# DeltaNet and MLP on one core: a new written order of all steps, decodes that wait for both transfers, and an early square root

## The chip, the cores and the metric

The kernel runs on one core of a Trainium2 chip. The time is the device time of one execution in microseconds. Its engines are TensorE (PE, matrix products; PEld are its weight loads), VectorE (DVE), ScalarE (ACT), GpSimd (POOL) and SyncE (SP); SP, ACT and POOL also issue DMA transfers. Each engine runs its instructions in the order in which the program holds them.

## What is computed

Two blocks follow each other. The first is a DeltaNet recurrence over 768 positions for 4 x 8 heads of 48 dimensions; the second is a layer norm and a two-layer MLP with a residual, on rows of 384 numbers.

```
k_n = k / (np.linalg.norm(k, axis=-1, keepdims=True) + 1e-06)
for t in range(S):
    y[:, :, t] = np.einsum('bhd,bhde->bhe', q[:, :, t], state)
    v_old = np.einsum('bhde,bhd->bhe', state, kt)
    state = state + bt * np.einsum('bhd,bhe->bhde', kt, vt - v_old)
...
x = attn_out.transpose(0, 2, 1, 3).reshape(B, S, H * D)
xn = (x - mu) / np.sqrt(var + 1e-06) * g_ln
out = x + np.maximum(xn @ w_ch1, 0.0) @ w_ch2
```

All data is float32. q, k, v and beta come in as (4, 8, 768, ...); w_ch1 is 384 x 1536, w_ch2 is 1536 x 384.

## The kernel before

**Tiling.** The 768 positions are cut into 12 chunks of 64. In a chunk the recurrence is a product with the inverse of a triangular 64 x 64 matrix, one for each of the 32 heads, and the state is carried from chunk to chunk. Chunk c has a recurrence (`recur`, tag c0, c1, ...) and then an MLP over its 256 rows (`mlp`, tag m0, m1, ...). Chunks 2 and 3, 4 and 5, and so on get their inverses in pairs by a substitution on VectorE (`rows_inverse`, tags x1, x2, ...; half of chunk 1 likewise, tag x0). From chunk 3 on, PE runs the MLPs with fewer products, whose sums are made on DVE, ACT and POOL.

**The start.** Chunk 0 cannot wait for VectorE's substitution: `first_inverse` makes its inverse on PE by doubling, in five levels, each for two groups of heads. A level has a product E (L771, with `qt` and `gsb`), a masked copy of E on DVE (L776), a product Z (L786, with `xt`), a transpose of Z on DVE (L735), and three back copies of Z on ACT (L729); the next E needs the transposes, the next Z the back copies. Ahead of them the keys of chunk 0 (`kr`, four transfers) are squared on ACT (L654), summed (L655) and rooted (L656) for the norms, turned on PE (L628), copied on ACT (L633) and multiplied with each other (L695). The results of E and Z go in turn to the PSUM tiles `two`, `by`, and the pair f0 and f1. After the inverse come the recurrence of chunk 0 (L1069, L1074, L1095), its output copy (L1133), the layer norm (L1139 to L1189), and the first product of the MLP, L1407. Gram products (L819) for chunks 1, 2 and 3 and the queries lie in between.

**Weights.** Both weight matrices come as pairs of 32-bit words and are put together on the chip. A piece is fetched by two transfers of 384 KB each, issued by ACT (`fetch`, keys "wd"), into one of five buffers (`words`, or a part of `h_all`). `convert` then decodes it in four operations: ACT scales the high words (L584), DVE shifts them (L589), ACT scales the low words (L592), POOL adds (L602). There are 12 pieces; the first three are decoded in two halves, which stand half by half in the two transfers.

**The order.** The function first records some 2,900 steps (`add`: engine, a cost, a closure, the keys it reads and writes). Then `emit` goes through ORDER, a list of step numbers written into the file, and emits each step as it comes; it only asserts that a step's inputs were emitted before. So ORDER alone sets the order on each engine, and the transfers' too: those that SP and ACT issue take their turns with eight semaphores in ORDER's order, so that one must have landed before the eighth after it can be issued. An "f" in ORDER is a filler: a product of zeros into the upper half of bank f0 (`zeros`, L1582). The three fills at the beginning (L617) are steps.

Of the kernel before, what the change touches and what calls it, by code (L numbers as in the profile page):

```python
# [131 lines left out]
47 9 6 257 8 48-49 10-11 13 1 32 26 23 14 0 12 65 7 66 60 39-43 256 45-46 44 61 55 74 53-54 52 58-59 327 56-57 63  # L132
405 408 64 37 21 5 17 30 71 35 73 69 75 238 79-80 82 85-86 96 89 88 36 29 15-16 20 4 18-19 90 33 97 87 91-92 3 93
98-99 83 100 94 84 101 81 106 104-105 103 76 38 27 95 102 124 22 125 118 126 239 119 24 77 108 70 107 109-110 215 78
226 127 111 122 121 112 129 72 246 123 240 128 213 133 25 134 120 f f 130 31 114 28 131-132 f f 135-137 141 115 2
142-143 222 139 138 140 147-150 216 145 230-231 146 144 157 151 116-117 214 159 153 152 158 209-210 163 250 154-155
161-162 160 156 211 164 113 401 403 314-316 412 260 325 67 313 326 265 410 259 262 68 264 263 266 261 413-414 328
407 409 212 f f 168 165 227 166-167 248 232 218 172-173 171 174 318 228 178 249 170 169 175-176 317 180-183 241 233
229 217 251 320 177 319 179 242 244 267 224 234 f 185 321 184 186 191 268-269 50 192 34 270-271 187 273 258 272 638
245 193 274-279 219 280 f f 197 243 322 370 329 323 188 195 330 189-190 331 194 196 247 369 332 363 650 652 399 199  # L140
198 200-201 205 333 204 364 202-203 206-207 334 208 335 f f f f 339 337 281-290 235 223 291-296 338 297-298 340 299
252 300-301 51 302-303 62 640 225 469 400 f 341-342 371 343-344 361-362 236-237 642 654 347 253 348 365 352 f f 435
434 402 324 404 336 411 304 474 477 406 476 475 307 305 767 309-310 312 308 311 306 437 436 345-346 353 372 349-351
354 220 373 367 221 374 f f f 438 355 359 439 360 366 440 415 357-358 356 478 577 575 254 578 581 479 368 255
480-482 418 416 473 484 643 641 637 644 656 649 655 639 653 768-769 771 773 772 770 766 419 576 375-376 579 614 420
580 583-584 379 377 582 388 381-382 421 485-503 422 504-509 378 510 423 511 645 587 615 585 616-617 387 588 591 424
586 592 428 427 426 595-596 425 417 380 651 589 429 441 599 618-619 442 774 512-523 394 430 433 431 590 383 432 393
443-444 385 389 445 593 524-526 390 657 527-528 448 446-447 384 529 600-602 646 908 449-450 391 397 395 1052 1054
1064 386 530 453 531 454 451-452 392 1066 603 647 604 658 620-621 594 458 455 605-606 597 607 659 456 532-533 459
534 460 457 461 465-466 464 467-468 463 462 598 622-623 608 396 535 483 398 1068 1065 536-539 629 540 630 541 631  # L150
542-543 632 544-547 633 609 778 775 805 624 610 625 806 910 912 763 907 911 764 914 901 648 913 660 909 900 662 1160
663-665 915 776 548 1056 1051 1057 1055 666 765 906 661 611 626 667-670 672 1162 550 549 551 903 552 628 627 673-674
902 905 1163 904 1165 1157 1167 613 811-812 807 777 809 817 810 818 675-677 815 808 816 823 821-822 824 813-814 1070
1069 829 832 830 833 1067 1053 678 779 679-690 553 691-701 554-558 838 819 702-704 634 705-706 564 707-711 559 827
839-840 562 561 560 563 828 820 780 841-842 848-849 843 781 712 1063 831 835 845 836 713 784 782 714 565 786 785 567
844 789 787 783 790 834 1058 825 850 715 788 568 826 794 791 566 569 795 716-717 796 792 718-719 793 720 855-856
851-852 865 916 853-854 801 797 570 866 846 873 867 837 802 799 804 574 572 571 800 573 803 798 917 721 1059 1526
847 1525 918 722-723 920 724 635 725-728 857 868 874-875 869 876 919 921 870 858 877 859-860 729-730 636 731-735
1347 1166 1348 1155-1156 1164 612 1168 736 1169 922-923 871 861 880-883 671 924 1071 1060 878-879 925 1061 1072
471-472 470 862 1528 1538 1170 1161 863-864 954 948 1073 927 891-893 956-957 884 894 872 926 895 962 896 1171 897  # L160
885 960 930-931 935 963 968 928 936 929 1540 1530 949 1075 951 950 739-740 1352 1062 1074 737-738 1077 1076
1078-1079 1172 886 969 961 932 937 741 1173 742 745-746 1080 958-959 743 974-975 744 887-888 955 980 953 933 952 752
1175 939 934 1081-1084 1087 1086 1529 1541 1531 1527 1537 1539 1532 1088-1091 938 1092-1104 966 989 747 967 749 964
748 965 751 972 990-993 750 973 970 1174 753 971 978 976 979 999-1001 994-995 1176 977 755-756 754 757 1177 1354 899
1356 889 898 890 1351 1345 1353 1158 940 1344 1159 941 1346 942 944 1357 943 1355 1006-1008 981 986 996 1016 1002
1009 1003 1010 983-984 982 1204 985 1203 987-988 1542 998 997 1014 1004 1017 1011 758 761 759 947 945 1178 1180 1018
1105-1109 1085 1110-1117 1005 1118-1119 946 762 760 1630 1358-1359 1637 1211 1120-1121 1179 1639 1629 1640-1641 1349
1122-1126 1024-1026 1212 1027-1029 1213 1019-1021 1030 1022 1543 1013 1023 1012 1182 1360 1031 1127 1350 1222 1015
1218 1185 1128 1361 1186 1129 1205 1226 1042 1032-1033 1043 1034-1036 1362 1130 1181 1190-1191 1183 1223 1037 1215
1044-1047 1216 1363 1184 1364 1131 1365 1132 1192 1133 1187 1214 1048 1217 1039 1206 1544 1366 1219 1227 1224 1220  # L170
1367 1369 1245 1230 1246 1231 1207-1208 1221 1533 1188 1134 1194 1189 1193 1368 1135 1225 1545 1232 1228 1534 1239
1233 1038 1209 1264 1259 1254 2026 1210 1240 1229 1535 1241 1234 1136 1242 1137-1138 1243 1247-1248 1250 1249 1251
1244 1139-1140 1252 1141-1142 1546 1265 1255 1266 1143-1145 1253 1547 1195 1643 1197 1642 1536 1636 1198 1638 1196
1049 1040 1199 1050 1548 1146 1267 1147-1148 1260-1261 1256 1149 1257 1262 1258 1202 1268 2028 2014 1273 1269
1235-1236 1292 1270 1293 1237 1274 1276 1271 1644 1275 1282-1283 1238 1272 1201 1277 1279 1403 1399 1289 1278 1280
1284-1288 1263 1200 1294 1645 1299-1302 1295-1297 1303-1304 1041 1150 1549 1298 1317 1309 1318 1553 1552 1829 1551
1550 1290 1392 1281 1305 1396 1310 1319-1320 1554 1291 1307 1306 1311 1321-1322 1312 1555 1646 1556 1308 1313-1314
1393 1557 1315 1558 1561 1323 1394 1316 1560 1407 1830 1828 1633 1151 1822 1154 1153 1152 1831 1833-1834 1832 2120
1835 1634 1324-1329 1335-1337 1330 1338-1339 1397 1340 1400-1401 1562-1563 1370 1372 1564-1565 1371 1566 1373-1376
1341 1377 1395 1408-1409 1379 1410 1402 2027 1635 1567 1404 1380 1568-1570 1378 1571 1405 1658 1416 1411 2015 1435  # L180
1445 1381 1423-1424 1572 1398 1406 1420-1421 1412 1426 1413-1414 2030 1427 1440 2029 1331-1332 2013 2016-2017 1422
1573 1647 1574 1382 1415 1648 1431 1651 1650 1649 1652 1428 1432 1429-1430 1575 1383 1425 1576 1660 1577 1433
1578-1580 1436 1653 1656 1654-1655 1441 1417 1442 1437 1446 1581 1447 1582 1418 1448 1438 1657 1449 1439 1659
1661-1662 1419 1450 1454 2025 1457 1455 1443 1583 1836 1343 1384 1334 1385 1387 1631 1333 1632 2125 1386 2126 1463
1451 1464-1468 1452 1584-1588 1453 1458-1459 1456 1460 1665 1663 1589 1469 1444 1434 1473-1475 1461 1470-1471 1462
2118 2117 1388 1342 2122 2124 2121 1821 2127 1390 1389 1391 1590 1480 1476-1477 1481 1478 1591 1664 1839 1592 1479
1472 1593-1595 1559 1482-1484 1498-1499 1490 1500-1501 1491-1493 1485 1502 1494-1495 1487 2032 2018 1596-1598 1496
1599 1688 1837 1503 1505-1507 1600 1486 1838 1699 1497 1827 1695 2031 1488-1489 2019 1666 1504 1668 1667 1601-1602
1689 1508-1509 1692 1510 1516 1690 1603 1511 1670 1669 1671 1840 1842 1604 1850 1696-1697 1517-1518 1693 1707 1703
1708 1731 2020 1675 1843-1844 1672 1841 1691 1845 1519-1521 1704-1705 1846 1849 1847-1848 1851 1706 1698 1605 1852  # L190
1606-1608 1676 1853-1854 1694 1673 1609-1612 1677 1522 1679 1674 1613-1614 1678 1615 1700-1702 1616 2021 1719-1720
1824 1826 1825 2129 2119 1823 1855 1680 2128 1512 1722 1741 1513 1709 1716 1710 1723 1736 1717-1718 1856 1617-1618
# [1537 lines left out]
```

## Time and profile before

| what | us |
|---|---|
| runs of the kernel | 529.24 median, 527.1 to 530.44 |
| the profiled execution | 530.82 |
| its span, first to last instruction | 529.1 |
| its granted PE clock | 0.976 of full |
| first product of the keys (L695) | 17.87 |
| first Z of the inverse (L786) | 29.74 |
| second Z, last group starts | 35.12 |
| third Z, first group | 42.56 |
| fifth Z, last group starts | 58.94 |
| first output copy of chunk 0 (L1133) | 65.75 |
| first MLP product (L1407) | 75.18 |
| last PE product ends | 524.7 |

How to read the lines that follow in the prediction. On the page, a line of an engine gives its busy time, its share of the span and its instructions. The rows of digits cut the span into 40 slices of 13.2 us; each digit is a busy share in tenths (9 is 90% or more), and PEclk is the clock that PE was granted, in tenths. The chain of waits follows the work that ended last back to the beginning; in order of time its lines give start, length, and what it was. A line of the waits gives who waited for whom, the sum, how often, and the longest. A line of the timeline gives start, length, engine, line of the code, operation, output and inputs, shape, how many; in brackets stands the idle time before it and what ended it.

### The profile page before, as it was taken

How to read it: one execution, taken by the hardware profiler on the slowest of the kernel's cores; microseconds unless marked ns; L12 is line 12 of the kernel's file. 1: busy time of each engine (PE TensorE's matmuls, PEld its weight loads, DVE VectorE, ACT ScalarE, POOL GpSimd, SP SyncE). 2: the span in 40 equal slices, each digit the busy share in tenths (PEclk: the TensorE clock that was granted, in tenths of full speed). 3: DMA queues.
4: the chain of work that ended last, by engine and by line, in shares of the span. 5: the costliest groups of instructions: out<-in, count | busy, mean ns of one | idle time of the engine just before them, and what ended most of it. 6: DMA issues, size and time to landing. Idle time of an engine off the chain costs nothing.

```text
span 529.1 us, 22717 instructions
## 1 busy us (share of the span) xinstructions
PE 496.1 (94%) x9938; PEld 451.6 (85%) x9938; DVE 358.6 (68%) x819; ACT 207.2 (39%) x451; POOL 284.3 (54%) x447
## 2 busy tenths in 40 slices
PE   5667988999999999989999999999999999999996
PEld 2455776767888889979999999999999999999996
DVE  2547778878997599986899954998837436354241
ACT  1786562542442334233261452353423424424130
POOL 7004485447245967767649437346374362554644
PEclk9588899999999999999999999999999999999999
DMA  9876759749543893159357267234343502102011
GB/s 178 200 161 122 211 89 233 118 121 164 101 69 81 178 156 55 35 147 191 60 120 135 48 184 126 45 85 75 97 100 71 117 4 60 34 33 59 1 32 30
DMA packets 181635, 54.56 MB, mean 103 GB/s; under 512 B 164888, under 2 KB 177312, under 8 KB 181536
## 3 DMA queue, kind: packets, MB, share of 16 engines
q1 hardware_dynamic: 168512, 40.10, 37.9%
q10 hardware_dynamic: 10816, 9.83, 6.7%
q0 software_dynamic: 2208, 3.17, 3.6%
q8 instruction: 78, 1.28, 1.0%
q14 instruction: 21, 0.17, 0.1%
HBM read 36.30 MB, written 16.78 MB: 100 GB/s over the span
## 4 chain that ended last, share of the span: by engine, by line
PE 85%; DVE 5%; issue 3%; DMA 2%; ACT 2%; SPq 1%; ACTq 0%; POOL 0%; DVEq 0%
PE f L1504 28%; PE f L1307 22%; PE f L1407 9%; PE two L819 3%; PE f L1429 3%; PE f L1582 2%; PE by L1033 2%; PE by L1095 2%; PE two L1088 2%; PE two L1033 2%; PE two L1105 2%; DVE xb L914 1%; DMA words<-in_moe_w_ch_dram 1%; SPq L401 1%; DMA kr<-in_k_dram 1%
## 5 line engine op out<-in xcount | busy, mean ns | idle before, releaser
L1504 PE MATMUL f<-w_sb,h_all 128*128 128x192 f32 x396 | 81.8, 329 | 0.0
L1491 POOL TENSOR_TENSOR h_all<-h_all 128x256 f32<-128x256 f32 x99 | 72.9, 753 | 14.9 <-DVE tmp L907 6.1
L1504 PE MATMUL f<-words,h_all 128*128 128x192 f32 x396 | 78.4, 330 | 0.1
L1330 DVE TENSOR_TENSOR h_all<-f,h_all 128x512 f32<-128x512 f32 x72 | 49.1, 686 | 33.3 <-PE f L1307 25.4
L1529 POOL TENSOR_TENSOR words<-h_all 128x128 f32<-128x128 f32 x66 | 31.2, 491 | 70.0 <-ACT h_all L1334 34.2
L1504 PEld LDWEIGHTS f<-w_sb,h_all 128*128 128x128 f32 x396 | 65.3, 190 | 1.1 <-POOL h_all L1491 0.2
L1504 PEld LDWEIGHTS f<-words,h_all 128*128 128x128 f32 x396 | 64.8, 190 | 1.4 <-issue 0.2
L914 DVE TENSOR_TENSOR xb<-xb,tmp 128x31 f32<-128x31 f32 (+19 forms) x139 | 58.8, 423 | 3.1
L907 DVE TENSOR_TENSOR tmp<-xb,gb 128x31 f32<-128x31 f32 (+19 forms) x139 | 53.0, 381 | 4.0 <-POOL xb L894 0.6
L1407 PE MATMUL f<-xnt,w_sb 128*128 128x256 f32 x216 | 52.6, 391 | 0.3 <-issue 0.3
L1325 ACT COPY h_all<-f 128x512 f32<-128x512 f32 x45 | 26.0, 586 | 58.8 <-PE f L1307 41.0
L401 POOL DMA_DIRECT2D tb<-in_k_dram x64 | 42.0, 660 | 13.0 <-DVE xb L914 7.4
L1334 ACT ACTIVATE h_all<-h_all 128x512 f32<-128x512 f32 x54 | 32.3, 625 | 36.2 <-DVE h_all L1330 36.0
L1407 PEld LDWEIGHTS f<-xnt,w_sb 128*128 128x128 f32 x216 | 40.4, 192 | 7.0 <-ACT h_all L1416 0.4
L1307 PE MATMUL f<-x_new,w_sb 128*128 128x128 f32 x288 | 39.8, 277 | 1.3 <-DVE h_all L1330 1.1
L1307 PE MATMUL f<-xnt,w_sb 128*128 128x128 f32 x288 | 40.7, 277 | 0.0
L1522 DVE TENSOR_TENSOR o<-f,x 128x192 f32<-128x192 f32 x33 | 11.6, 354 | 41.7 <-PE f L1504 24.9
L602 POOL TENSOR_TENSOR w_sb<-words 128x768 uint32<-128x768 uint32 (+1 forms) x11 | 15.0, 1365 | 43.3 <-DVE words L589 33.4
L1307 PEld LDWEIGHTS f<-x_new,w_sb 128*128 128x128 f32 x288 | 36.7, 192 | 1.7 <-issue 1.5
L1307 PEld LDWEIGHTS f<-xnt,w_sb 128*128 128x128 f32 x288 | 37.1, 191 | 0.3
L1133 ACT COPY x<-by 128x384 f32<-128x384 f32 x23 | 10.4, 481 | 53.2 <-POOL o L1522 36.3
L1416 ACT ACTIVATE h_all<-f 128x256 f32<-128x256 f32 x36 | 13.4, 383 | 35.1 <-PE f L1407 34.9
(252 smaller groups left out, 987.4 us busy)
## 6 DMA issues: line engine op xcount, KB each, us to landing
words<-in_moe_w_ch_dram ACTq DMA_DIRECT2D x20, 384.0 KB, 4.6
gd<-gsb SPq DMA_DIRECT2D x11, 512.0 KB, 3.9
v<-in_v_dram SPq DMA_DIRECT2D x24, 192.0 KB, 3.9
kr<-in_k_dram SPq DMA_DIRECT2D x46, 96.0 KB, 3.6
out_dram<-o SPq DMA_DIRECT2D x46, 96.0 KB, 2.3
xld<-xlt SPq DMA_DIRECT2D x9, 384.0 KB, 2.5
xnt<-xld SPq DMA_DIRECT2D x36, 96.0 KB, 3.0
tb<-in_q_dram SPq DMA_DIRECT2D x40, 64.0 KB, 2.9
```

The lines of the kernel that those rows point to most:

```text
L401: add(eng, cost, lambda: QUEUE[eng].dma_start(out=out_, in_=in_), r, w, bulk=n * ns / 16e3, np=n, **kw)
L907: lambda j=j, n=n, w=w, t=t: nc.vector.tensor_tensor(out=t, in0=xv[:, 0:n, j : j + 1].to_broadcast([128, n, w]), in1=gv[:, j : j + 1, j + ...
L914: "DVE", dve(n * w), lambda t=t, rest=rest: nc.vector.tensor_tensor(out=rest, in0=rest, in1=t, op=ALU.subtract),
L1033: nc.tensor.matmul(dst[half(e), hp, j], src[drows(hp), (e if n else key_half(c, hp, e)) * GP + j], s_all[drows(hp), e, j], start=(n == 0 o ...
L1307: nc.tensor.matmul(wide(p[:, f : f + 128]), w[:, f : f + 128], r, start=start and i == 0, stop=True, skip_group_check=True)
L1325: add("ACT", act(512), lambda: nc.scalar.copy(o, p), pk, ok)
L1330: add("DVE", dve(512), lambda: nc.vector.tensor_tensor(out=o, in0=x, in1=y, op=op), [*xk_, *yk], ok)
L1334: add("ACT", act(512), lambda: nc.scalar.activation(o, o, ACTF.Relu, scale=scale), [], ok)
L1407: nc.tensor.matmul(p[:, 0:TOK], w1_sb[:, t, f * 128 : (f + 1) * 128], xnt[:, t], start=(t == 0), stop=(t == KC - 1))
L1491: add(eng, cost, lambda: e.tensor_tensor(out=out_, in0=x, in1=y, op=op), r, w, port=2 if eng == "Pool" else 1, pr=-2)
L1504: lambda f=f, t=start and f == order[0]: nc.tensor.matmul(p[:, 0:D2], lhs(f), rhs[:, f], start=t, stop=(f == order[-1]), skip_group_check=True
L1529: lambda f=f + i: e.tensor_tensor(out=s3[f], in0=one(0, 0)[0](f), in1=one(1, 0)[0](f), op=ALU.subtract),
```

## The change

Three things change in the recorded steps. The memset of `eps` and its square root, a step whose only use is that ACT loads its table, are recorded first, and the first steps on ACT that don't issue a transfer now need it (key "act"). A decode needs both transfers of its piece, also where it decodes one half. And ORDER is another list.

```
+    c_dve(lambda: nc.vector.memset(eps, 1e-6), 0.06, ["eps"])
+    add("ACT", 1.48, lambda: nc.scalar.sqrt(rstd[:, 0, 0:1], eps), ["eps"], [("ln", 0, 0), "act"], t0=2.2)
     c_dve(lambda: nc.vector.memset(nought, 0.0), 0.2, ["nought"], pr=-300)
...
                     "ACT", act(512), lambda o=o: nc.scalar.copy(o, eye[:, None, :].to_broadcast([128, H, C])),
-                    ["eye"], [(*key, x) for x in range(2)],
+                    ["eye", "act"], [(*key, x) for x in range(2)],
...
-    c_dve(lambda: nc.vector.memset(eps, 1e-6), 0.06, ["eps"])
-    add("ACT", 1.5, lambda: nc.scalar.sqrt(rstd[:, 0, 0:1], eps), ["eps"], [("ln", 0, 0)], t0=2.2)
...
-        wk = WORD_KEYS[BUF[i]] + [("wd", BUF[i], c0 // 384 + y) for y in range(n // 384)]
+        wk = WORD_KEYS[BUF[i]] + [("wd", BUF[i], y) for y in range(2)] + ["act"]
...
-            add("ACT", act(512), lambda o=o, i=i: nc.scalar.copy(o, i), pair[2 + g], [dkey + (g,)], **kw)
+            add("ACT", act(512), lambda o=o, i=i: nc.scalar.copy(o, i), [*pair[2 + g], "act"], [dkey + (g,)], **kw)
...
-            add("ACT", act(384), lambda sq=sq, s=s: nc.scalar.square(sq, kn[:, s]), raw_keys(0), kg, **kw)
+            add("ACT", act(384), lambda sq=sq, s=s: nc.scalar.square(sq, kn[:, s]), [*raw_keys(0), "act"], kg, **kw)
```

Each engine keeps the same operations, but ACT has one load of its function table where it had two, and there are 17 fillers where there were 19. What the new order holds, as far as the prediction speaks of it:

- ACT: the four key transfers (two from ACT, two from SP) are the first four; then the square root, the two squares, a fetch, an eye copy, a root, two eye copies, a root, a fetch, the two key copies of chunk 0, three fetches, an eye copy, four fetches with a small copy among them, the two key copies of chunk 1, the six back copies of the first level with two small copies, a fetch and a half decode among them. Before, a fetch stood between ACT's two key transfers, and four fetches and the first half decode stood ahead of the squares.
- ACT after the first Z: gram copy, half decode, gram copy, three back copies of the first group, a whole decode, a small copy, a half decode, a back copy, a half decode, two back copies.
- PE after the first key products: two fills, the turns of chunk 1's keys, two fillers, half a gram product, E, the other half, E, Z, a turn of the queries, Z, three fillers, E of the second level, a turn, E, a filler, Z, Z. A filler also stands ahead of the third Z, ahead of the gram product at the fifth level (behind a back copy that reads f0), and two stand behind the fifth Z.
- POOL: the fetch of the first beta rows and one more stand ahead of the iotas that VectorE's masks begin with. The decodes of the first layer's fifth and ninth parts stand behind a memset of the second inverse's tile (L872) and the scaling of v of chunk 1.
- PE at the MLP of chunk 0: the state product of chunk 1 (L1033), which stood ahead of the MLP's first group, stands behind its second.
- DVE and ACT at the layer norm of chunk 0: one decode step each lies among its steps, where there were several.

## Prediction

> **What bounds the kernel now.** I read the page first: busy shares, slices, the chain of waits.
>
> ```profile
> PE 496.1 (94%) x9938; PEld 451.6 (85%) x9938; DVE 358.6 (68%) x819; ACT 207.2 (39%) x451; POOL 284.3 (54%) x447
> PE   5667988999999999989999999999999999999996
> PEclk9588899999999999999999999999999999999999
> PE 85%; DVE 5%; issue 3%; DMA 2%; ACT 2%; SPq 1%; ACTq 0%; POOL 0%; DVEq 0%
> ```
>
> PE is the bound, except in the first six slices (13.2 us each): there it is half busy and its clock is down. PE's idle time by stage is 11.1 us in 0 to 20, 4.9 in 20 to 40, 3.5 in 40 to 60, 2.5 in 60 to 80. From 75.18, where the MLP of chunk 0 starts (L1407), PE's waits sum to 7.1 us up to 524.7, 4.7 of it "issue" (the engine waited for nothing that the profile shows). Behind PE's last product lie 4.4 us. The change lays out the same products anew, so it can win only before 75.18, and lose anywhere. Next, the chain of waits in order of time, and ScalarE's waits:
>
> ```profile
> 3.22 5.25 DMA kr<-in_k_dram
> ...
> 9.10 5.86 DMA words<-in_moe_w_ch_dram
> ...
> 15.43 0.92 ACT xln L654 x2
> ...
> 36.48 2.60 issue
> ...
> 53.11 2.07 PE f L1582 x4
> ```
> ```profile
> ACT words L584 <- DMA words<-in_moe_w_ch_dram: 5.5, 1, 5.5
> ACT kt L478 <- DMA kr<-in_k_dram: 4.1, 1, 4.1
> ```
>
> ScalarE runs in order. A fetch waits 4.1 us for its place (a key transfer must land first); then a decode of weights waits 5.5 us for its transfer, with the squares (L654) and key copies (L633) behind it. So the key products (L695) begin only at 17.87, though the keys were there by 8.5. Fillers (L1582, zero products) are 16% of the chain up to 76. They write bank f0 and wait for its readers too, and PE is in order:
>
> ```profile
> 17.87 1.13 PE L695 MATMUL by<-kt 48*64 48x64 f32 x32 [5.72 <-ACT kt L633]
> ...
> 29.74 0.69 PE L786 MATMUL by<-xt,gsb 64*64 64x64 f32 x32
> ...
> 53.11 2.07 PE L1582 MATMUL f<-u 128*128 128x256 f32 x4 [2.67 <-DVE qt L735]
> 55.12 1.13 PE L771 MATMUL two<-qt,gsb 64*64 64x64 f32 x32
> ```
>
> **The change, stage by stage.** Operations are the same but for one table load (1.28) and two fillers. The sums use this execution: span 529.1, its own time 530.82, the median of the runs 529.24. I carry the difference to the median.
>
> Start to L695. The square root of eps now needs DVE's memset at about 3.2, which the load of the table covers (2.92 to 4.2); the second load (17.84, ahead of the key norms) goes. The four key transfers come first on both queues; before, a 384 KB fetch lay between them. POOL issues two small fetches (0.72, 0.65) ahead of the iotas, so DVE begins at 3.1, not 2.38; with 15 short operations the pads of the keys end at 5.7. ScalarE: squares to 6.6; the fetch behind them waits for a key transfer issued at 3.5 (3.6 median to land) and ends at 7.6; three eye copies 1.8, two roots 0.3, a fetch 0.3, two key copies 1.15. L695 at 11.1: -6.8. If the fetches wait here as before (4.1), -2.7.
>
> L695 to the first Z (L786): 11.87 now. PE's new queue there, at full clock from the first fills on: two products 2.13, four fills 3.78, transposes 1.1, two fillers 1.0, gram halves and E 2.1: 10.1. ScalarE is later: eight fetches and copies up to L695+6.3, then two key copies 1.15, six copies of the first level 2.34, two small ones 0.4, a half decode 0.56, a fetch: 10.95 in all: -0.9. At half clock PE needs 14.2: +2.3. Granted clock was 0.50 from 17 to 29 through 11 us of nearly gapless small products; but the four fills at 4.39 took 3.78 and the transposes at 9.76 ran at 0.14 each, against 0.28 at half clock. The new queue holds those fills, so I take the nearer row. The Trainium skill (TensorE: Matmul & The Clock Gate, Part 1) says that any busy window of some 3.4 us opens the clock; the small products here contradict it with 11 us at 0.50. By that rule this stage would come out at -0.9 too, by the small products at +2.3.
>
> First Z to the end of the second Z: 6.06 now (29.74 to 35.8). Three fillers stand ahead of the second level's E, and ahead of them in f0 stands ScalarE's last back copy. ScalarE has queued from the first Z on: two gram copies 1.2, a half decode 0.56, three copies 1.16, a whole decode 0.96, 0.2, then three copies mixed with two half decodes 2.25: 6.35, where three copies would be 1.16. PE then has a gap of 4.9 us. A gap of 2.67 at 53.11 cost it half its clock, so the fillers take 3.1, then E 1.06, transposes and E 1.0, a masked copy 0.75 (a filler beside it) and Z 1.15. Sum 13.4: +7.3. If they didn't hold E back, only Z's last half would wait for the copies: 7.7, +1.6. I take 7.3: the wait at 53.11 is just this.
>
> Second Z to third: 6.76 now, of which 2.60 "issue" and 2.07 fillers. ScalarE's new queue gives 3.5 (six copies, a query copy, a decode, a filler). The issue stall may come again at the same place in PE's code: -3.3 without, -0.7 with; taken at -2.0.
>
> Third Z to the end of the fifth: 17.07 now. New: ScalarE up to the fourth Z 7.6 (five decodes 3.2, nine copies), Z 1.0, then 4.0 to a filler's f0 copy, filler 0.5, gram 1.05, E 0.5, fillers 1.0, Z 1.1: 16.8, -0.3. The fourteen fetches on ScalarE here count little: at 48.35 one lay wholly beside a decode. Z's end to the first output copy (L1133): 6.12 now, 5.7 new, -0.4.
>
> Output copy to 75.18: 9.43 now; DVE's and ScalarE's decodes lie inside the layer norm (L1145 waits behind two decodes, 1.5), and the query mask (1.23) ahead of xnt. New: two copies 0.96, one decode 0.92, roots 0.6, state copy 0.8, query copies 1.07, xnt 0.9, turns and mask-free waits 1.9: 7.1, -2.3. In return the first state product (L1033, 1.15) stands behind two MLP groups: +1.15 of PE's work left.
>
> The rule on both transfers: a 384 KB transfer lands after 4.4 (median), and the first such decode stands some 8 us behind the later of its two fetches: I cost the extra wait at nothing. Were that cover gone it would cost ScalarE up to 5.5 again, with the back copies behind it. POOL's decode of the fourth group now stands behind a scale of v and a memset that waits for a transfer of the small inverse (L872): four to five us to spare, nothing.
>
> Sum: -6.8 -0.9 +7.3 -2.0 -0.3 -0.4 -2.3 +1.15 = -4.25. Behind it PE has the same work and, I assume, the same 7.1 us of waits, give or take 2. From 529.24: 525.0.
>
> **Rivals.** (1) The fillers hold nothing back (the E's inputs end last, or the clock stays up): +1.6 instead of +7.3, 519.3. For it: E needs only DVE's transposes, ready early. Against: at 53.11 the filler itself waits. (2) The start does not do what it says: ScalarE's fetches wait for their places, as now (4.1): 529.1. For: nine fetches are queued within 7 us and DMA is 94% busy up to 20. (3) Slower: every fetch that ScalarE issues holds it for its whole 0.55 (at 50.53, with nothing to lie beside, the next copy came 0.64 later). Fourteen lie in the inverse, 0.45 more each: 6.3. With the issue stall whole (1.3), half clock up to the first Z (1.4 of the 3.2, the rest beside ScalarE) and after the gap that it makes at the fifth level (filler and gram twice as long, 1.5) it is 10.5: 535.5. It decides where fetches follow each other, as eight do ahead of the second key copies; against it stand 48.35 and 57.76, where they cost 0.1.
>
> **How the numbers follow.** The forecast (start won, about 40% kept, 521 to 529) has 0.44; rival 1 0.30, rival 2 0.12, rival 3 0.14. About 1% (5.3 us) is what the measurement can tell from no change. Of the forecast's 0.44, 0.11 lies below 523.95; with rival 1 faster is 0.41. Same is 0.33 and rival 2: 0.45; slower is rival 3. Range: low 518 (rival 1 with a little less waiting later), high 533, which leaves out most of rival 3. Likeliest 525.0, its own range 521 to 529.
>
> **What would show it.** L695 near 11; one table load; no ScalarE wait for weights; a PE wait of some 5 us on ScalarE at a filler (L1582) near 28, with the clock at 0.50 after it; the MLP's first group near 70. I am wrong if L695 comes behind 14, if the second Z ends before 32, or if PE's waits from the MLP on sum to over 10 us.

## The result and the profile after

| | before | changed |
|---|---|---|
| median of the runs, us | 529.17 (527.1 to 530.44, 4 runs) | 521.67 (518.49 to 525.85, 4 runs) |
| profiled execution, us | 530.82 | 522.44 |
| its span, us | 529.1 | 520.7 |
| granted PE clock | 0.976 | 0.989 |

The ratio is 0.9879, with a 95% interval of 0.9839 to 0.9919: the changed kernel is faster by 1.2%, or 7.5 us between the medians. The two profiled executions are 8.4 us apart; the sums below are made between these two, as the prediction's were. The profiled execution of before lies high: 23 further runs of that kernel lay between 523.17 and 531.51.

The four lines of the page that stand for the ones shown of before:

```profile
PE 491.3 (94%) x9934; PEld 447.7 (86%) x9934; DVE 350.0 (67%) x819; ACT 205.5 (39%) x450; POOL 282.4 (54%) x447
...
PE   4577799999999999999999999999999999999997
...
PEclk9989799999999999999999999999999999999999
...
PE 87%; issue 3%; DMA 2%; ACT 2%; DVE 2%; SPq 1%; POOL 1%; ACTq 0%; DVEq 0%; POOLq 0%
```

PE is nine tenths busy from the sixth slice on, as before from the eighth, and the first five are no fuller. What fell in the chain is VectorE, from 5% to 2%. Next the waits ahead of 72 us, by who waited for whom (sum, times, longest):

```profile
PE f L1582 <- ACT xt L729: 7.4, 4, 3.1
...
PE two L771 <- issue: 2.7, 1, 2.7
...
PE f L628 <- DMA kr<-in_k_dram: 1.8, 1, 1.8
...
ACT gsb L480 <- DMA kr<-in_k_dram: 1.1, 1, 1.1
```

Up to the MLP no decode on ScalarE waits for weights any more, and no fetch ahead of the key copies waits for its place. (Behind them some do: the longest wait is 2.3 us, ahead of the fetch at 15.65, until the last key transfer has landed at 15.63.) In place of that PE waits: 7.4 us in fillers (L1582; each filler is two products in the profile) for ScalarE's back copies, 2.7 for nothing that the profile shows, 1.8 for the keys of chunk 1. The same in order of time on PE (start, length, line, what; in brackets the idle time ahead and what ended it):

```profile
10.79 0.87 PE L695 MATMUL two<-kt 48*64 48x64 f32 x32
...
15.88 1.06 PE L628 MATMUL f<-ident,kr 128*128 128x128 f32 x8 [1.82 <-DMA kr<-in_k_dram]
...
22.53 0.33 PE L771 MATMUL two<-qt,gsb 64*64 64x64 f32 x5 [2.71 <-issue]
22.65 0.69 PE L786 MATMUL by<-xt,gsb 64*64 64x64 f32 x32
...
27.69 2.38 PE L1582 MATMUL f<-u 128*128 128x256 f32 x6 [3.13 <-ACT xt L729]
30.00 1.13 PE L771 MATMUL by<-qt,gsb 64*64 64x64 f32 x32
...
59.39 2.07 PE L1582 MATMUL f<-u 128*128 128x256 f32 x4 [2.56 <-ACT xt L729]
...
71.51 1.78 PE L1407 MATMUL f<-xnt,w_sb 128*128 128x256 f32 x7
```

By the prediction's stages, with both landmarks read from the two timelines of PE (and of ScalarE for L1133):

| stage, us | before | after | forecast | measured |
|---|---|---|---|---|
| start to L695 | 17.87 | 10.79 | -6.8 | -7.1 |
| to the first Z | 11.87 | 11.86 | -0.9 | 0.0 |
| to the end of the second Z | 6.06 | 12.21 | +7.3 | +6.1 |
| to the third Z | 6.76 | 4.02 | -2.0 | -2.7 |
| to the end of the fifth Z | 17.07 | 17.95 | -0.3 | +0.9 |
| to the first output copy | 6.12 | 7.52 | -0.4 | +1.4 |
| to the MLP of chunk 0 (L1407) | 9.43 | 7.16 | -2.3 | -2.3 |
| sum up to the MLP | 75.18 | 71.51 | -5.4 | -3.7 |
| from there to PE's last product | 449.5 | 445.35 | +1.15 | -4.15 |
| from PE's last product to the end of the run's time | 6.1 | 5.6 | 0 | -0.5 |

So in these two executions half of the gain is where the prediction put it, and as much comes from behind the MLP's start, where it had put a small loss.

### The profile page after: what moved, and what is told of

The parts are those of the page before. It is cut to its first block, busy times and chain, and to the rows that moved or that the text cites. A ratio compares the mean times of both kernels' runs of the same rounds, so it can differ in the third digit from the quotient of the medians.

```text
span 520.7 us, 22708 instructions
## 1 busy us (share of the span) xinstructions
PE 491.3 (94%) x9934; PEld 447.7 (86%) x9934; DVE 350.0 (67%) x819; ACT 205.5 (39%) x450; POOL 282.4 (54%) x447
## 3 DMA queue, kind: packets, MB, share of 16 engines
q8 instruction: 78, 1.28, 1.0%
## 4 chain that ended last, share of the span: by engine, by line
PE 87%; issue 3%; DMA 2%; ACT 2%; DVE 2%; SPq 1%; POOL 1%; ACTq 0%; DVEq 0%; POOLq 0%
PE f L1504 28%; PE f L1307 24%; PE f L1407 10%; PE two L819 4%; PE f L1429 3%; PE by L1095 2%; PE two L1033 2%; PE by L1033 2%; PE two L1088 2%; PE two L1105 2%; DMA kr<-in_k_dram 1%; PE f L1582 1%; SPq L401 1%; ACT xt L729 1%; DMA xd<-xb 1%
## 5 line engine op out<-in xcount | busy, mean ns | idle before, releaser
L1504 PE MATMUL f<-w_sb,h_all 128*128 128x192 f32 x396 | 80.4, 330 | 0.3 <-POOL h_all L1491 0.3
L1504 PE MATMUL f<-words,h_all 128*128 128x192 f32 x396 | 76.4, 328 | 0.0
L1504 PEld LDWEIGHTS f<-w_sb,h_all 128*128 128x128 f32 x396 | 64.8, 190 | 1.6 <-POOL h_all L1491 0.8
L1504 PEld LDWEIGHTS f<-words,h_all 128*128 128x128 f32 x396 | 65.3, 190 | 0.5 <-POOL h_all L1491 0.2
L914 DVE TENSOR_TENSOR xb<-xb,tmp 128x31 f32<-128x31 f32 (+19 forms) x139 | 53.5, 385 | 3.1
L907 DVE TENSOR_TENSOR tmp<-xb,gb 128x31 f32<-128x31 f32 (+19 forms) x139 | 50.7, 365 | 4.5 <-POOL xb L894 1.2
L1407 PE MATMUL f<-xnt,w_sb 128*128 128x256 f32 x216 | 51.7, 387 | 0.0
L1407 PEld LDWEIGHTS f<-xnt,w_sb 128*128 128x128 f32 x216 | 39.6, 190 | 6.6 <-ACT h_all L1416 0.4
L1307 PE MATMUL f<-xnt,w_sb 128*128 128x128 f32 x288 | 40.8, 277 | 0.0
L1307 PE MATMUL f<-x_new,w_sb 128*128 128x128 f32 x288 | 40.2, 278 | 0.0
L1307 PEld LDWEIGHTS f<-xnt,w_sb 128*128 128x128 f32 x288 | 37.2, 191 | 0.4
L1307 PEld LDWEIGHTS f<-x_new,w_sb 128*128 128x128 f32 x288 | 36.5, 191 | 0.4
L1504 PE MATMUL f<-w_sb,words 128*128 128x192 f32 x132 | 26.6, 329 | 0.2 <-issue 0.2
```

What stands on the lines that cost most here:

```text
L907: lambda j=j, n=n, w=w, t=t: nc.vector.tensor_tensor(out=t, in0=xv[:, 0:n, j : j + 1].to_broadcast([128, n, w]), in1=gv[:, j : j + 1, j + ...
L914: "DVE", dve(n * w), lambda t=t, rest=rest: nc.vector.tensor_tensor(out=rest, in0=rest, in1=t, op=ALU.subtract),
L1307: nc.tensor.matmul(wide(p[:, f : f + 128]), w[:, f : f + 128], r, start=start and i == 0, stop=True, skip_group_check=True)
L1407: nc.tensor.matmul(p[:, 0:TOK], w1_sb[:, t, f * 128 : (f + 1) * 128], xnt[:, t], start=(t == 0), stop=(t == KC - 1))
L1504: lambda f=f, t=start and f == order[0]: nc.tensor.matmul(p[:, 0:D2], lhs(f), rhs[:, f], start=t, stop=(f == order[-1]), skip_group_check=True
```

## The experiments

Each run is given by its ratio to the kernel before on the same chip, since that kernel's median there lay between 527.3 and 528.2. The edits are in ORDER alone; no filler is part of the result, so none leaves computation out. "L695", "L1407" and "L1407 to PE's last" are read from each run's one profiled execution. In before, e1, e2 and e7 the state product (L1033, 1.15 us) lies ahead of L1407, in the others behind it, within the last column.

| run | median, us | ratio, 95% interval | L695 | L1407 | L1407 to PE's last |
|---|---|---|---|---|---|
| before | 529.17 | 1 | 17.87 | 75.18 | 449.5 |
| changed | 521.67 | 0.9879, 0.9839 to 0.9919 | 10.79 | 71.51 | 445.4 |
| e5 changed again | 521.26 | 0.9888, 0.9839 to 0.9937 | 10.79 | 71.96 | 445.1 |
| e1 new until MLP | 529.54 | 1.0044, 1.0019 to 1.007 | 10.79 | 74.20 | 449.3 |
| e2 new from MLP | 524.32 | 0.9939, 0.9907 to 0.997 | 23.03 | 74.47 | 444.1 |
| e7 state product first | 522.81 | 0.9908, 0.9875 to 0.9942 | 10.79 | 73.84 | 442.5 |
| e6 old start | 522.18 | 0.9896, 0.9848 to 0.9943 | 16.42 | 71.87 | 444.5 |
| e3 no three fillers | 516.56 | 0.9812, 0.977 to 0.9854 | 10.79 | 66.70 | 444.5 |
| e4 no waiting fillers | 515.38 | 0.9772, 0.9731 to 0.9813 | 10.34 | 66.28 | 442.8 |
| e8 no fillers | 517.75 | 0.9809, 0.9761 to 0.9857 | 10.61 | 70.62 | 443.0 |
| e9 copies first | 519.12 | 0.9851, 0.9824 to 0.9878 | 10.79 | 70.70 | 442.6 |
| e10 old start, no waiting fillers | 517.51 | 0.9817, 0.9787 to 0.9848 | 16.49 | 65.37 | 443.1 |
| e11 late fetches | 514.79 | 0.9773, 0.9741 to 0.9804 | 10.54 | 69.18 | 442.6 |
| e12 put together | 513.47 | 0.9736, 0.97 to 0.9771 | 10.78 | 64.38 | 443.5 |

### Which half of the order: e1, e2 and e5

```
e1:  ORDER = new[: first L1407] + [s for s in old if s not in new[: first L1407]]
e2:  ORDER = old[: first L1407] + [s for s in new if s not in old[: first L1407]]
     (steps that need the early square root stand behind it)
```

> The new order up to the first product of the MLP of chunk 0 (L1407), behind it the steps in the old order's sequence. In the two profiles the MLP starts 3.7 us earlier (71.51 against 75.18), of which 1.15 us is a state product (L1033) that the new order puts later; here it stands ahead of the MLP again. Theory, the gain has two halves, and the one behind the MLP's start belongs to the order there: the MLP starts near 72.7, PE waits some 7 us from there on as in the kernel before, time 526.5 (2.6 below the kernel before). Rival, all of the gain comes from the beginning, because earlier decodes and fetches also take away the later waits: PE waits 4 us or less behind the MLP's start, time 522.

> The old order up to the first product of the MLP of chunk 0, behind it the steps in the new order's sequence. Theory, the order behind the MLP's start brings its own 5.9 us (3.5 of PE's waits, 1.7 of half clock near 104, the rest at the end): time 523.5, PE's waits behind 75 some 4 us. Rival, the waits behind the MLP's start are a matter of the beginning: time 529, waits 7 us. Second rival, those waits differ from run to run whatever the order: the time lies anywhere between, and the single waits (L819, L949, L1052) have other places than in either kernel.

> The changed kernel once more, on the same chip as the three that follow. If the order behind the MLP's start sets the waits there, PE waits some 4 us in all from 72 on and less than 1 us in the stretch from 200 to 250 (2.85 idle in the kernel before); if they are a matter of the run, 7 us. Time 521.7, give or take 2.

In one point e2 isn't what its expectation says. The new steps let ScalarE compute only after the square root, and the old sequence has that behind ten fetches of weights; so its key products begin at 23.03, 5 us later than in the kernel before. The fillers need no such step, and 13 of the 19 run ahead of the key products, none in the inverse:

```profile
14.24 5.83 PE L1581 MATMUL f<-u 128*128 128x256 f32 x26
```

(Lines of e2 are lower by one: L1581 is L1582.) So e2 tests the order from the MLP on behind a beginning that is neither kernel's.

With the new order up to the MLP and the old one behind it, nothing is gained: 1.0044, with the interval above 1. Neither time of its expectation was met; e2's 524.32, with 4.1 us of waits behind the MLP's start, lies near its first theory's. PE's waits behind 72 us in e1:

```profile
PE f L944 <- DVE xnj L938: 3.2, 1, 3.2
PE two L1033 <- DVE pt L850: 1.4, 1, 1.4
PE two L819 <- issue: 1.1, 1, 1.1
PE f L1307 <- DVE h_all L1330: 1.1, 1, 1.1
PE f L1504 <- DVE o L1522: 0.6, 1, 0.6
```

And in the changed kernel run again (e5):

```profile
PE f L944 <- DVE xnj L938: 0.9, 1, 0.9
PE by L1095 <- issue: 0.9, 2, 0.6
PE two L819 <- issue: 0.7, 1, 0.7
PE by L949 <- issue: 0.5, 1, 0.5
```

The waits for VectorE of 1.1 (L1307) and 0.6 (L1504) and the stall of 1.1 at L819 lie between 200 and 250. They stand in the kernel before, too, and the two for VectorE in none of the kernels with the new order there. The window from 200 to 250 us in the kernel before, in e1 and in the changed kernel (start and length, then busy time and instructions of PE, PEld, DVE, ACT and POOL, granted clock, DMA share, GB/s):

```profile
200.00:250.00 50.00, 47.15 (x1063) 44.68 (x1055) 41.38 (x76) 17.63 (x37) 36.34 (x54) 1.00 0.49 105
200.00:250.00 50.00, 47.18 (x1026) 44.72 (x1019) 40.78 (x77) 17.06 (x35) 36.41 (x54) 1.00 0.50 108
200.00:250.00 50.00, 49.82 (x1090) 47.44 (x1089) 39.02 (x83) 17.67 (x36) 41.49 (x62) 1.00 0.60 124
```

PE is busy 49.64 us of it in e5 and 48.90 in e2. So this piece, 1.7 to 2.7 us, goes with the order behind the MLP's start, and for it the rival falls that the waits go with the run. For the rest it doesn't. The 3.4 us at half clock near 104 in the profile of before are not in e1, which has the same order there; that piece, some 1.7 us (PEclk 0.57 from 104 to 108), is one of that execution. PE's stalls without a releaser sum to 4.7 us in the kernel before and to 1.3 in e1 under the same order (2.8 in the changed kernel), so they don't follow this order alone.

The last column of the table seems to say more: 449.3 to 449.5 us with the old order from the MLP's start to PE's last product, 442.5 to 445.4 with the new one. But the 449.5 hold the 1.7 at half clock, and the 449.3 of e1 hold what its seam costs: the wait of 3.2 at L944, which is 0.3 in the kernel before, and half clock behind it (0.50 from 82.73 to 86.14). Without these pieces they would be some 447.8 and 444.7, against 444.1 (e2) and 442.5 (e7) with the new order and the state product likewise ahead.

The two halves don't add: +2.3 us for the one, -3.0 for the other, some -6.5 for both. The mixed orders have waits at their seam that neither kernel has in this size (L944 and L1033 in e1), and e2 has a beginning of its own; so they don't say what the new beginning alone is worth.

### The state product: e7

```
- ... 639 473 577 575 440 254 ...      (577, 575: L1407; 440: L1033)
+ ... 639 473 440 577 575 254 ...
```

> The changed kernel with one product of the state (L1033, 1.15 us) back ahead of the MLP of chunk 0, on PE alone; all else stands. The prediction took its place for neutral: time 521.7. Theory now, from the wait of 1.42 us for VectorE's masked gram (L850) that L1033 has ahead of the MLP in the mixed kernel: it waits here too, and the MLP starts 2.6 us later, time 523.1.

```profile
72.76 1.15 PE L1033 MATMUL two<-s_all,kt 48*64 48x48 f32 x64 [1.42 <-DVE pt L850]
73.84 2.86 PE L1407 MATMUL f<-xnt,w_sb 128*128 128x256 f32 x12
```

The wait came, and the MLP starts 1.9 us later than in e5 (71.96). But the time, 522.81, can't be told from 521.26, and PE's last product even ends earlier in the profile (516.32 against 517.02): the product's later place only moves a wait, since L944 then no longer waits 0.9 us for VectorE. Neutral, as the prediction had it. It also means that of the 3.7 us by which the MLP starts earlier, some 2 (1.9 against e5, 2.3 against the changed kernel's first profile) are this product and its wait.

### What the early start is worth: e6 and e10

```
e6, e10: ORDER = old[: first L695] + [s for s in new (e10: in e4) if s not in old[: first L695]]
         (steps that need the early square root stand behind it)
```

In both, ScalarE begins with the old sequence's first five fetches of weights and the key transfers; then come table load, square root, squares and key copies, with no decode ahead of them. The expectation of e6 speaks of a half decode there; it needs the square root, too, and so comes later. L695 comes at 16.42, 1.4 us ahead of the kernel before. Behind the first key product all stands as in the changed kernel (e10: as in e4).

> The changed kernel with the beginning of the kernel before, up to the first key product (L695): ScalarE's fetches and its first half decode stand ahead of the squares again, the rest is in the new order's sequence. The changed kernel reaches L695 7.1 us earlier than the kernel before (10.79 against 17.87). Theory, what is lost there is lost to the end: L695 near 17.9, MLP near 78, time 528.5. Rival, the later waits of PE for ScalarE's back copies take up half of it, since ScalarE has then done decodes that stand ahead of those copies: MLP near 74.5, time 525.

> The changed kernel without the seven fillers that wait (515.4), and with the beginning of the kernel before up to the first key product (L695). With the fillers the early start was worth 0.9 us in time, though L695 came 5.6 us earlier. Theory one, the fillers masked it: without them the old beginning costs 3 us or more, 518.5. Theory two, two other things take it up ahead of the first Z, the wait for the keys of chunk 1 and the issue stall, which a late start passes without waiting: first Z at 24.7, 1.7 later than without, and 516 to 517.

PE's timeline in e6:

```profile
16.42 1.13 PE L695 MATMUL two<-kt 48*64 48x64 f32 x32 [3.15 <-ACT kt L633]
...
18.34 1.97 PE L628 MATMUL f<-ident,kr 128*128 128x128 f32 x8
...
24.71 0.69 PE L786 MATMUL by<-xt,gsb 64*64 64x64 f32 x32
...
30.01 2.93 PE L1582 MATMUL f<-u 128*128 128x256 f32 x6 [3.40 <-ACT xt L729]
```

The key products are 5.6 us later than in the changed kernel, the first Z 2.1, the MLP 0.4 (0.1 earlier than in e5). The times can't be told apart (522.18 against 521.26). Neither number of the expectation was met: the late start costs nothing like 7, and not 3. What takes the 5.6 us up is to be seen in the bracketed waits: in the changed kernel PE stands 1.82 us for the keys of chunk 1 at 15.88 and 2.71 at 22.53; in e6 it passes both places without a wait. That takes up 3.5 us by the first Z. Most of the rest goes from the fourth level on: e6 has no stalls there (0.49 and 0.28 in the changed kernel), and its clock is up again sooner behind the last fillers (L1095 takes 0.68 a group, 1.10 in the changed kernel). Without the seven fillers the old beginning costs 2.1 us by the medians (517.51 against 515.38; the intervals overlap), and its one profile reaches the MLP earlier, at 65.37. (That execution was the fastest of its six, 514.09.) So the early start is worth between nothing and 2 us by the medians, with or without the fillers. e2 can't be counted here: with L695 at 23.03 it begins the recurrence of chunk 0 (L1069) at 57.46, before the changed kernel's 61.39, but its inverse holds no fillers.

### The fillers: e3, e4 and e8

```
e3:  - ... 226 145 144 f f f 149 ...          + ... 226 145 144 149 ...
e4:  the same, and the f behind 156, the f behind 234, and both f behind 217
e8:  no f
```

> The changed kernel without the three fillers (L1582) ahead of the second level's E. Theory, they hold E back behind a back copy of ScalarE (wait of 3.13 us, then 2.38 at half clock): E starts near 26.3 rather than 30.0, the second Z ends near 30.5 rather than 34.86, the first product of the MLP comes 3 us or more earlier, time 518.5 (3 below the changed kernel). Rival, E's own inputs or the clock take the place of the fillers (E at half clock too, ScalarE's decodes behind it hold the third Z): the second Z ends 1 us earlier at most, time 521.

> The changed kernel without the seven fillers that wait for ScalarE's copies: the three of the run before it, one ahead of the third Z (0.81 us of wait), one ahead of a gram product at the fifth level (0.93), two behind the fifth Z (2.56, then 2.07 at half clock). Theory, each of them is in the way: the recurrence of chunk 0 (L1069) starts 2 us sooner behind its last copies, the MLP 5 to 6 us earlier than 71.51, time 516. Rival, without them PE is idle longer, the clock is at half for more of the small products, and what is saved in fillers is lost there: MLP at 70 to 72, time 519 to 522.

> The changed kernel without any of the 17 fillers. Against the kernel without the seven that wait (515.4): theory one, the ten that are left keep PE's clock up, and without them more small products run at half clock: 517 to 519, more 3.4 us stretches at half clock before the MLP. Theory two, they only take PE's time, 0.5 us each where PE is the last: 512 to 514, MLP 1.5 to 3 us earlier than 66.28.

PE in e3, without the three ahead of the second level's E:

```profile
26.39 1.13 PE L771 MATMUL by<-qt,gsb 64*64 64x64 f32 x32 [1.77 <-DVE qt L735]
...
31.16 0.69 PE L786 MATMUL two<-xt,gsb 64*64 64x64 f32 x32
...
55.92 1.20 PE L1582 MATMUL f<-u 128*128 128x256 f32 x4 [2.56 <-ACT xt L729]
```

E waits for VectorE's transposes alone and starts at 26.39 instead of 30.00; the second Z ends at 31.85 instead of 34.86. The median falls by 4.7 to 5.1 us against the two measurements of the changed kernel (the intervals overlap by 0.0015), and the MLP starts 4.8 us earlier, more than the 3 that this stage gives: the fillers behind the fifth Z wait 2.56 us as they did, but then take 1.20 instead of 2.07, because the clock was still up when they began (it fell at 56.86, 0.94 us later). That is half of the other 1.8. In e4 the recurrence (L1069) starts at 54.63, 2.4 us before e3's, but then it waits for the copies itself, and the MLP comes only 0.4 earlier. At 0.9772 it can't be told from e3; both are clearly below the kernel before, by 1.9 and 2.3%.

The other ten are of use. The window from 20 to 40 us in e8, which has none (busy time and instructions by engine, then granted clock, DMA share, GB/s):

```profile
20.00:40.00 20.00, 14.10 (x392) 12.35 (x390) 9.46 (x22) 13.91 (x31) 3.12 (x6) 0.50 0.74 165
```

and in e4:

```profile
20.00:40.00 20.00, 13.82 (x513) 11.56 (x508) 11.24 (x27) 16.52 (x38) 5.91 (x7) 0.91 0.70 162
```

PE is as busy, but at half clock it gets through 392 products instead of 513; the MLP starts at 70.62, 4.3 us behind e4's. The time, 517.75, is 2.4 above e4's by the medians, with intervals that overlap. The granted clock of all executions says it more clearly: 0.960 to 0.976 in the six of e8, 0.987 to 0.993 in the five of e4. So the profile bears out theory one of e8's expectation, and theory two falls.

### What makes the fillers wait: e9

```
- ... 142 137 246 214 238 146 226 145 144 f f f ...
+ ... 142 137 146 145 144 246 214 238 226 f f f ...
```

> The changed kernel with all its fillers; on ScalarE alone, two and a half decode steps and a small copy that stand among the back copies behind the first Z (L592, L671, L584 twice: 1.9 us) move behind the last of those copies. Theory, the decodes make the three fillers wait, and the wait also closes the clock: the last back copy ends near 25.8 instead of 27.64, the wait falls from 3.13 to 1.2 us, the fillers run at full clock in 1.5 instead of 2.4 to 2.9, the second Z ends 2.5 to 3 us earlier, time 518 to 519. Rival, the fillers hold E whatever stands on ScalarE, because they follow each other on PE: only 1 us is won, 520.5.

ScalarE in e9:

```profile
23.06 1.15 ACT L729 COPY xt<-by 64x256 f32<-64x256 f32 x3 [0.30 <-PE by L786]
26.31 1.14 ACT L729 COPY xt<-f 64x256 f32<-64x256 f32 x3 [2.10 <-DVE qt L735]
27.35 0.89 ACT L592 ACTIVATE words<-words 128x768 uint32<-128x768 uint32 x1
```

and PE:

```profile
27.50 2.93 PE L1582 MATMUL f<-u 128*128 128x256 f32 x6 [2.52 <-ACT xt L729]
```

The decodes are gone from between the copies, and the copies still end near 27.4: by the profile their second half starts only when VectorE has done its transposes of the same Z. The wait at the filler falls from 3.13 to 2.52, so the decodes made 0.6 us of it. (The Z ended 0.4 later here, and the filler starts 0.2 earlier.) The time, 519.12, lies 2.1 below e5 with intervals that overlap. In the profile the second Z ends no earlier than in e5 (both at 35.7), and the MLP starts 1.3 us earlier; what of that belongs to the decodes isn't shown.

### Two versions: e11 and e12

```
e11 (on e4): 76 73 (fetches of weights) from ahead of 87 (a key copy) to behind it,
             72 78 (fetches) from ahead of the first level's copies to behind 138
e12 (on e4): 76 73 and 72 so; 246 214 238 226 (decodes) behind 144,
             244 245 behind 156, 224 behind 202 (decodes behind the last back copy)
```

> The changed kernel without the seven fillers that wait (515.4), and four of ScalarE's fetches of weights (384 KB each) later: two from ahead of the key copies of chunk 0 to behind them, two from ahead of the first level's back copies to behind those of the first Z. Theory, these transfers delay the keys of chunk 1 (wait up to 2.6 us before 16) and the transfer of PE's instructions (issue stall of 1.2 to 2.8 before the first Z): chunk 1's keys are there 2 us earlier, the stall is under 1.2, the first Z starts near 20.5 instead of 22.96, time 513.5. Rival, the stall or VectorE's chain ends where it did, or a decode now waits for its late transfer: first Z within 1 us of 22.96, time 515 to 516.

> A version put together from the runs: the changed kernel without the seven fillers that wait, with three of ScalarE's fetches later (two behind the key copies of chunk 0, one behind the first back copies of the first Z), and with the decode steps that stand among the back copies of the first, second and fifth Z moved behind them. Theory, each gives a little more (third Z 0.8 us, recurrence of chunk 0 0.55 us): MLP at 66 or earlier, time 513. Rival, what is won before the fifth level is lost again there to issue stalls and half clock, as in the version with late fetches (first Z 4.1 us earlier, time 0.6 less): 514 to 515.5.

PE in e11:

```profile
13.46 1.03 PE L628 MATMUL f<-ident,kr 128*128 128x128 f32 x8
...
18.72 0.33 PE L771 MATMUL two<-qt,gsb 64*64 64x64 f32 x5 [0.42 <-issue]
18.84 0.69 PE L786 MATMUL by<-xt,gsb 64*64 64x64 f32 x32
...
55.22 0.59 PE L786 MATMUL two<-xt,pt 64*64 64x64 f32 x11 [1.96 <-issue]
```

The cause was met, the time was not. With fewer large transfers ahead of them the keys of chunk 1 are there without a wait, and the stall shrinks from 1.23 in e4 to 0.42: the first Z starts at 18.84, 4.1 us before e4's. By the E of the fourth level it is lost: that begins at 39.70, in e4 at 39.68, and e11 had run at half clock from 23.76 to 40.83, where e4 did so for 3.4 us. Two stalls of 1.25 and 1.96 in the fifth level and half clock from 54.48 to 64.72 put it behind e4. This profile is of the slowest of its six runs (517.39); the median, 514.79, is that of e4 within the interval.

e12 is the fastest of all, 0.9736, and lies below both kernels of the change: 513.47 against 521.67. In its profile, PE:

```profile
21.33 0.69 PE L786 MATMUL by<-xt,gsb 64*64 64x64 f32 x32 [1.24 <-ACT xt L729]
...
48.07 0.35 PE L771 MATMUL two<-qt,gsb 64*64 64x64 f32 x9 [1.40 <-issue]
```

The stall in the fifth level is there again, but the MLP starts 1.9 us before e4's. Against e4 alone, 1.9 us by the medians, the intervals overlap (0.97 to 0.9771 and 0.9731 to 0.9813).

## Why the prediction was right, and where it was not

It forecast 525.0 (518 to 533) and the time was 521.67: it had the direction, and 4.2 of the 7.5 us. By the number, rival 1 (519.3) is nearer; that the fillers do hold PE back is read from the trace. Point by point:

- **Start to L695 (-6.8).** Right in size (-7.1): no wait for weights, one table load, four keys first. But the sum carried it on as 40% of a gain that is kept, and e6 shows next to none: L695 5.6 us later, and the same time within what can be told. It is a landmark more than a cause. One reading was wrong and cost nothing: the table load didn't cover VectorE's memset, the square root waited 1.08 us for it, and the squares then waited 1.25 for the keys anyway.
- **To the first Z (-0.9).** Measured 0.0. The sum walked PE's and ScalarE's queues and left out two waits: for the keys of chunk 1 (1.82) and the issue stall (2.71). The prediction had allowed for the stall "at the same place in PE's code", behind the second Z; it came here. It also called the products of the kernel before, at half clock from 17 to 29, 11 us of small ones; some 3 us of them are fillers (2.07 from 24.46, 1.37 from 28.44).
- **First Z to the end of the second (+7.3).** The mechanism is the one forecast, and rival 1 (the fillers hold nothing back) falls: PE waited 3.13 us at a filler and ran at half clock behind it, and e3, without the three, ends this stage 3.0 us earlier. The size came out at +6.1; the gap was put at 4.9. ScalarE had the two gram copies and a half decode done before the first Z, while PE stood in the stall, so the last copy ended 5.0 behind the Z's start and not 6.35. The reason given was partly wrong, too: the copies were counted late because of ScalarE's decodes, and e9 shows that the decodes make 0.6 of the 3.13, while VectorE's transposes hold the copies anyway.
- **To the third Z, and to the MLP (-2.0, -2.3).** Measured -2.7 and -2.3. The second size was met for another reason than the one summed. The layer norm did get shorter: its last scaling on VectorE (L1189) ends 4.5 us behind the first output copy's start, where it ended 8.4 behind it. But in e7, with the state product back ahead of the MLP, the stage takes 9.65 (64.19 to 73.84), against 9.43 in the kernel before. So what this stage gains is the product that moved out and its wait for VectorE's query mask; that the sum has the same number is luck. The two stages in between are 3 us worse than forecast: two stalls (0.49, 0.28), and behind the fifth Z two fillers that wait 2.56 and run at half clock, with the recurrence of chunk 0 (L1069, L1095) at half clock behind them. The prediction named these fillers in the order, and gave them no price.
- **The state product (+1.15 left for later).** Neutral in time, as costed; e7.
- **Both transfers for a decode (nothing).** Up to the MLP no decode on ScalarE waits for weights in the changed kernel. The rule acts only through the list, since emit just asserts it.
- **Behind the MLP, "the same 7.1 us of waits, give or take 2".** This is the step that failed. PE's idle time fell from 6.84 to 3.16, the half clock near 104 (1.7) is not there, and with 1.15 more work the stretch is still 4.15 shorter. Of these 5.3 us, e1 and e2 tie 2.7 to the new order's place for the steps between 200 and 250; 1.7 belong to the one execution of before; for the last 1, in stalls without a releaser, no run shows that the order is the cause. The step before it, "it can win only before 75.18, and lose anywhere", is wrong for the same reason: 7.1 us of waits can also be won.
- **Rivals 2 and 3.** Rival 2 fell: no fetch ahead of the key copies waited for its place, and the longest wait, 2.3 us at 15.65, lies where ScalarE's next key copies had to wait for the same keys. Rival 3 (each fetch holds ScalarE 0.55) fell too: of the fetches from 42 to 53 all but one lie beside ScalarE's other operations, and behind that one (50.73) 0.44 us is idle.

So the sum has two errors of opposite sign, 1.7 us too much won ahead of the MLP and 5.3 too little behind it. That the first makes up for a third of the second is luck, too.

The Trainium skill (TensorE: Matmul & The Clock Gate, Part 1) has a busy window of some 3.4 us open the clock. The stage of the first Z can't test this: its clock was up since the fills at 12.06 (four in 1.99 us) and stayed up. The kernel before speaks against it: PE was busy all the time from 18.89 to 22.29, with 89 products, and the granted clock was 0.50 until 29.12.

## What to carry to other kernels

A landmark that comes earlier is worth only what no later wait takes back: follow it to the next transfer and the next buffer that PE needs, and ask which of them would have been late anyway. A filler that keeps the clock up had better not write a buffer that another engine still reads; three such fillers cost some 5 us here by the medians, 3 of them in their own stage, while ten others kept the clock at 0.91 instead of 0.50 between 20 and 40 us. And where a list orders a whole kernel, the waits behind the stage that one looks at are part of what it can win.

## What the runs showed of the hardware

**PE's issue stalls stand at counts of products.** The page has 78 transfers and 1.28 MB in the queue of instructions, 16 KB each, for 9,934 products and as many weight loads: one for some 127 products. Up to the stall ahead of the first Z, in the changed kernel:

```profile
0.00:22.40 22.40, 11.11 (x221) 7.73 (x221) 11.94 (x50) 11.78 (x27) 11.22 (x26) 1.00 0.95 227
```

and in e4 up to the stall in the fifth level:

```profile
0.00:47.90 47.90, 30.68 (x855) 23.69 (x856) 29.37 (x103) 30.80 (x70) 16.85 (x33) 0.93 0.86 187
```

221 products are also done at this stall in e3 and e4, and 475 at the one of 2.60 us in the kernel before: 254 more, twice 127. 855 (e4 and e2, in different code) is five times 127 behind 221 within one, and 983 (e4's next) is six times. Behind the MLP's start the stall at L949 stands at 1,619 in the kernel before and at 1,621 in the changed one, eleven times 127 behind 221 within three. (One of 0.28, at 1,386 in the kernel before, fits no multiple.) So the place moves with what PE has done, not with the line. The transfer of that queue starts at 19.94 in the changed kernel, at 20.16 in e4, 16.08 in e11 and 36.41 in the kernel before, and PE goes on 2.6 to 2.7 us later each time (22.53, 22.83, 18.72, 39.08). That the stall is the wait for these instructions is inferred from this; e11, with four large transfers moved away, made it shorter (1.23 to 0.42), which fits.

**A wait of the same length did or didn't close the clock.** At the stall ahead of the first Z the changed kernel waited 2.71 us, and the products behind ran at full clock (0.69 for 32). In e5, the same kernel, it waited 2.74 and they ran at half:

```profile
22.17 0.37 PE L771 MATMUL two<-qt,gsb 64*64 64x64 f32 x3 [2.74 <-issue]
...
22.43 1.08 PE L786 MATMUL by<-xt,gsb 64*64 64x64 f32 x30
```

The granted clock shows why. In all 14 traces each stretch at half clock up to 100 us is 3.41 us long or a multiple of it (3.41 from 28.30 and 6.83 from 59.02 in the changed kernel, 13.65 from 15.47 in the kernel before). Cut into steps of 3.41 us from its first recorded change on, a trace closes the clock behind a step in which PE was busy for about half of it or less (0.03 to 0.53 in 32 of 33 cases, 0.62 in one), and in 270 steps that left it open PE was busy for 0.48 or more. The 2.71 us lay across two steps, with PE busy 1.77 and 2.03 us of them; the 2.74 us left 1.42 of one. The Trainium skill (the same page, Part 1) says that the window is free-running, so that its phase decides; these cases agree with that.

**One 96 KB transfer took twice its kind's median.** The last key transfer of chunk 1 took 7.37 us in the changed kernel, from 8.26, where the median of its kind on the page is 3.5. Fetches of 384 KB were under way then; in e11, with two of them behind ScalarE's key copies, PE turns these keys at 13.46 without a wait, and not at 15.88 after one.
